# The attention's linear part as one matrix per batch, with a new order of the instructions

## The chip, the cores and the metric

The kernel runs on one core of a Trainium2 chip. Its engines are PE (TensorE, matrix products), DVE (VectorE), ACT (ScalarE), POOL (GpSimd) and SP (SyncE, which here only issues DMAs). Each engine works through its own instructions in order; semaphores make one wait for another. The metric is the device time of one execution in microseconds (us), the median of several runs.

## What is computed

Attention over pooled keys is followed by a feed-forward layer. Keys and values are the same 768 vectors of each batch; there are 4 batches of 12288 queries with 128 channels.

```python
kv_pool = kv.reshape(B, H // r, r, W // r, r, C).mean(axis=(2, 4))
k = v = kv_pool.reshape(B, -1, C) @ w_sr
s = (q @ k.transpose(0, 2, 1)) / sqrt(C)
a = exp(s - s.max(-1)); a /= a.sum(-1) + 1e-09
x = (a @ v).reshape(B * S, D)
h = x @ w_in
out = (h - tanh(h)) @ w_out
```

## The kernel before

The scores are small, so the kernel writes exp(s) as 1 + s + r2 and sums the three parts apart. The keys are centred first, so the 1 sums to nothing but the mean, which is taken into constants; the part in s is a linear map of q, the matrix M of a batch (values times keys, `Mn`); only r2 needs the 768 keys. The feed-forward layer is likewise expanded about the batch's mean: a slope matrix A (128x128), and a remainder that comes from products with `winr` and `Wr`.

The queries are cut into 96 tiles of 512, 24 for each batch. `attention(g)` and `feed_forward(g)` issue one tile's work:

- three products of scores into wide PSUM buffers (`big`, 128x1024, three buffers, which all wide products share), each followed by ACT's exp (`E`) and DVE's r2 = E - 1 - s;
- the sum of r2 over the keys: SP copies the first r2 to `rs` (line 794), POOL's DMA queue adds the other two to it (line 797, called an add below), and PE sums over partitions (line 802); from that ACT makes the scale `t` (line 822);
- `num`, in the narrow PSUM bank `x`: six half-precision products of the values with r2 (line 818) and three products for the linear part, M high with the rounded q, M low with it, and M high with q's rest `ql` (line 808);
- DVE multiplies `num` by `t` to `df` (line 829), POOL rounds it to `dr` (line 832) and takes the rest `dl` (line 858). A high and low times `dr`, and A high times `dl`, go to the bank `acc` (line 878);
- eight wide products `dr` by `winr` (line 889). Seven of them go to ACT (square, `u`) and DVE (`r`); the eighth goes to ACT (copy, `v`) and then POOL (`z`, `z`, `rp`, lines 903 and 907). Sixteen products with `Wr` go to `acc` (line 927), ACT adds the constant and writes the result `o` (line 938), and SP stores it.

A tile of a batch's last part also carries a share of the next batch's preparation (`keys`, `about_centre`): the keys are gathered by 15 DMAs on POOL's queue that add to `kvp` (line 366, called gathers below), centred, multiplied; M, A, `winr` and `Wr` are made anew.

The order is written out by numbers: each operation has a step (tile start `8 g` plus an offset from the table `AT`), and a planner sorts each engine's operations by step, within the dependencies. `BUFS` says how many buffers each name has.

Of the kernel before, what the change touches and what calls it, by code (L numbers as in the profile page):

```python
# [21 lines left out]
P = 128  # L22
# [134 lines left out]
def attention_then_ffn(ctx: ExitStack, tc: tile.TileContext, q, kv_by_key, kv_by_place, w_sr, w_in,  # L157
# [76 lines left out]
    def words_of(step, load_step, n, kind):  # L234
# [55 lines left out]
        Y, M, part = (ym, "y"), (ym, "m"), (key, n)  # L290
        plan.op(load_step, "SP", 0.5, load_words, () if kind == "i" else ("held",), (words,), late=2.0,
# [13 lines left out]
    def weights(step, load_step):  # L305
# [3 lines left out]
        for j in range(2):  # L309
            turned = f"turned.{j}"  # L310
            big(turned, step + NW + j)
            for k in range(2):
                def turn(j=j, k=k, turned=turned):
                    for f in range(8 * j + 4 * k, 8 * j + 4 * k + 4):
                        PE.matmul(out=plan[turned][:, (f % 8) * P : (f % 8 + 1) * P],
                                  lhsT=win32[:, f * P : (f + 1) * P], rhs=ident,
                                  start=True, stop=True)

                plan.op(step + NW + j, "PE", 1.0, turn, (("win32", 2 * j + k), "ident"),
                        ((turned, k),), late=0.2)  # L320
# [4 lines left out]
            plan.op(step + NW + j, "ACT", 1.03, copy, (turned,), (("winT", j),), late=0.1)  # L325
        s = 16.0
        bank("WW", "x", s)
        sb("WW32", "W2", [P, P])
        bank("W4", "x", s + 1)
# [11 lines left out]
        norm(s + 1, "WW32", "W4", B)  # L341
# [13 lines left out]
    def keys(b, s0):  # L355
# [6 lines left out]
        NK = K // KB  # L362
        for w in range(W if b else 0):
# [6 lines left out]
            at = (b * NG - GATHER[b - 1] + max(w - 1, 0)) * UN + AT["more"][0] - 2 * UN  # L370
            plan.op(at - (0.01 if w else 4), *(("POOL", 0.87) if w else ("SP", 0.5)), gather, (), (kvp,),
                    late=3.0, dma=1.0, lane=w > 0)
        for j in range(0 if b else NK):
# [3 lines left out]
            at = slice(j * KB, (j + 1) * KB)  # L377

            def load(at=at, key=key):
                SP.dma_start(out=plan[key], in_=kv_by_key[:, at, :])  # L380

            plan.op(s - 8, "SP", 0.5, load, (), (key,), late=2.0, dma=1.27)
            if j % 3 == 2:
                for k, w in enumerate((8, 4, 2, 1)):
                    def fold(key=key, w=w, at=at):
                        x = plan[key]
                        to = plan[kvp][:, at].unsqueeze(2) if w == 1 else x[:, :, 0:w]
# [4 lines left out]
            else:  # L392
                def pool(key=key, at=at):
                    V.tensor_reduce(out=plan[kvp][:, at], in_=plan[key], op=ALU.add, axis=AX.X)
# [8 lines left out]
        Mh = f"Mh.{b}"  # L403
        sb(Mh, "Mh", [P, 2, C], R32)
# [3 lines left out]
        for x, at in ((pc, s0), (pm, s3), (p4, s4)):  # L408
            bank(x, "x", at)
# [66 lines left out]
        def copy_moment():  # L476
            A.activation(out=plan[Mn], in_=plan[pm][:, 0:P], func=AF.Copy, scale=scale)
            A.copy(out=plan[Mh][:, 0], in_=plan[Mn])

        def moment_left():  # L480
            PL.tensor_tensor(out=plan[Mh][:, 1], in0=plan[Mn], in1=plan[Mh][:, 0].bitcast(F32),
                             op=ALU.subtract)

        for n in range(NK // 2):
            of = (kvp,) if b else ((kvp, 2 * n), (kvp, 2 * n + 1))
            plan.op(s0 - 0.5, "DVE", 0.3, partial(part, n), of, ((row, n),))
        plan.op(s0, "DVE", 0.35, mean, (row,), (row,))
        plan.op(s0, "ACT", 0.85, apart, (kvp, row), (kvp,), late=0.1)
        plan.op(s0, "PE", 0.2, centre, ("wsr", row), (pc,), late=0.2)
        plan.op(s0, "DVE", 0.12, copy_centre, (pc,), (cen,))  # L490
        for c in range(2):
            plan.op(s1 + c / 4, "PE", 0.65, partial(product, c), ("wsr", kvp), ((pk, c),), late=0.2)
        plan.op(s1, "ACT", 0.9, copy_keys, (pk,), (kTr,), late=0.1)
        for j in range(2):
            plan.op(s2 + j / 4, "PE", 0.7, partial(product_by_key, j), ("wsr", kvp), ((pv, j),),
                    late=0.2)
        plan.op(s2, "ACT", 0.85, copy_values, (pv,), (vv32,), late=0.1)
        plan.op(s2 + (0 if b else 2), "DVE" if b else "ACT", 0.9, small_values, (pv,), (vvr,))
        plan.op(s3, "PE", 1.8, moment, (vv32,), (pm,), late=0.2)
        plan.op(s3, "ACT", 0.65, copy_moment, (pm,), (Mn, Mh), late=0.1)  # L500
        plan.op(s3, "POOL", 0.35, moment_left, (Mn, Mh), (Mh,))
        norm(s4, Mn, p4, b)

    def about_centre(b, s0):
# [9 lines left out]
        sb(Am, "A", [P, C])  # L514
        Ah = f"Ah.{b}"
        sb(Ah, "Ah", [P, 2, C], R32)
        sb(Wr, "Wr", [P, FT, C], R32)
        FS, CS, AS, APART, SA, TA, WI, WS = EARLY if b < 2 else LATER
        first_at = [s0 + FS * n if b else s0 - 9.9 + n / 4 for n in range(4)]
        known = s0 + 3 * FS + 2 if b else s0 - 9  # L520
        winr_at = known + WI if b else s0
        slopes_at = [known + SA + AS * n if b else n / 2 - SL for n in range(4)]
        third_at = [known + TA + AS * (n + 0.5) if b else n / 2 - THIRD for n in range(4)]
        for n in range(4):
            if b or n == 0:
                bank(f"{ph}.{n}", "x" if b else "acc", first_at[n])
            if b:
                bank(f"{pa}.{n}", "x", slopes_at[n] + APART)
        if not b:
            bank(f"{pa}.0", "acc", slopes_at[0])  # L530
# [49 lines left out]
        def inverse_of():  # L580
            h, z, p, g0, g1, a3, slope, y, inv = (x(n) for n in range(9))
            V.reciprocal(out=inv, in_=slope)
            V.tensor_reduce(out=stat[:, b : b + 1], in_=z, op=ALU.add, axis=AX.X)
# [644 lines left out]
```

## Time and profile before

| | us |
|---|---|
| median of 3 runs (1326.55 to 1327.71) | 1327.05 |
| span of the profiled execution | 1326.8 |
| busy PE | 1271.4 |
| busy DVE | 1220.6 |
| busy ACT | 1197.4 |
| busy POOL | 1143.5 |

A busy share is no distance from a limit here: PE's matmuls overlap, so that its busy time holds waits too. The execution is best read in stages, with the start of the result copies `o` as a clock, one for each tile:

| stages | us | tiles |
|---|---|---|
| up to the second `o` | 100.7 | 1 |
| gather stages (one gather in nearly every tile) | 125.7, 125.5, 163.1 | 10, 10, 13 |
| change stages (the next batch is prepared) | 149.6, 152.3, 150.3 | 10, 11, 11 |
| plain stages (neither) | 146.7, 122.2 | 12, 10 |
| a check of the expansion's limits, between the plain stages | 42.4 | 3 |
| the end | 48.3 | 4 and the rest |

### The profile page before, as it was taken

To read this page: it belongs to the slowest core of one execution; us is meant where nothing else is said; L and a number is where in the kernel's file an instruction comes from. 1 tells how busy PE (TensorE), PEld (TensorE's weight loads), DVE (VectorE), ACT (ScalarE), POOL (GpSimd) and SP (SyncE) were. 2 spreads that over 40 slices of the span, in tenths; PEclk is the share of its full clock that TensorE was granted. 3 is DMA by queue.
4 is the path that set the end of the run, shared out by engine and by line. 5 is a ranking of instruction groups with operands and counts; after the bars stand their busy time and mean duration, and the time that the engine had idled before them with its cause. 6 is when DMAs were issued, how large, how long until landed. Compare 5 with 4: busy or idle time off the path is not lost.

```text
span 1326.8 us, 17379 instructions
## 1 busy us (share of the span) xinstructions
PE 1271.4 (96%) x5520; PEld 889.0 (67%) x5520; DVE 1220.6 (92%) x1201; ACT 1197.4 (90%) x1423; POOL 1143.5 (86%) x969
## 2 busy tenths in 40 slices
PE   4899999899899999999999999999999999999997
PEld 3666666676666667766666666776767667667665
DVE  6789999788899999999899999999999999899996
ACT  4689999788899999899899999899899999899996
POOL 3587999779999988799999998799998889798896
PEclk8899999999999999999999999999999999999999
DMA  9255666436566654445566664444444444434431
GB/s 350 52 112 128 139 134 141 94 106 129 125 136 140 134 128 97 114 112 132 115 142 133 136 137 110 104 104 112 104 108 107 104 119 96 103 97 108 115 82 40
DMA packets 82708, 158.47 MB, mean 119 GB/s; under 512 B 9936, under 2 KB 12112, under 8 KB 82608
## 3 DMA queue, kind: packets, MB, share of 16 engines
q0 software_dynamic: 33552, 66.99, 30.8%
q1 hardware_dynamic: 49056, 90.29, 19.4%
q8 instruction: 45, 0.74, 0.2%
q14 instruction: 55, 0.45, 0.1%
HBM read 57.93 MB, written 25.39 MB: 63 GB/s over the span
## 4 chain that ended last, share of the span: by engine, by line
POOL 44%; PE 38%; ACT 6%; issue 6%; DMA 2%; DVE 2%; SPq 0%; POOLq 0%; ACTq 0%; DVEq 0%
PE acc L927 11%; POOL rp L907 11%; PE big L889 10%; POOL z L907 10%; POOL rs L797 6%; PE big L774 5%; POOL z L903 4%; PE x L818 4%; POOL ql L812 3%; POOL dr L832 3%; ACT E L778 3%; PE x L808 2%; PE acc L878 2%; ACT v L900 2%; POOL kvp L366 1%
## 5 line engine op out<-in xcount | busy, mean ns | idle before, releaser
L896 DVE SCALAR_TENSOR_TENSOR r<-big,u 128x1024 fp32r<-128x1024 f32 x672 | 778.9, 1217 | 27.9 <-ACT u L893 27.5
L893 ACT ACTIVATE u<-big 128x1024 f32<-128x1024 f32 x672 | 662.4, 1034 | 34.3 <-PE big L889 23.4
L889 PE MATMUL big<-dr,winr 128*128 128x512 f32 x1536 | 510.4, 413 | 1.7 <-DVE r L781 0.9
L927 PE MATMUL acc<-r,Wr 128*128 128x512 f32 x1344 | 426.8, 409 | 0.6 <-DVE r L896 0.6
L781 DVE SCALAR_TENSOR_TENSOR r<-E,big 128x1024 f16<-128x1024 f32 x288 | 350.2, 1217 | 51.1 <-ACT E L778 48.0
L889 PEld LDWEIGHTS big<-dr,winr 128*128 128x128 f32 x1536 | 276.5, 188 | 97.0 <-DVE r L781 25.8
L778 ACT ACTIVATE E<-big 128x1024 f32<-128x1024 f32 x288 | 296.0, 1029 | 19.9 <-PE big L774 9.7
L927 PEld LDWEIGHTS acc<-r,Wr 128*128 128x128 f32 x1344 | 251.8, 188 | 65.1 <-DVE r L896 1.5
L907 POOL TENSOR_TENSOR rp<-z,v 128x1024 fp32r<-128x1024 f32 x96 | 273.5, 2849 | 0.2
L907 POOL TENSOR_TENSOR z<-z,v 128x1024 f32<-128x1024 f32 x96 | 248.7, 2590 | 4.3
L797 POOL DMA_DIRECT2D rs<-r x188 | 223.7, 1190 | 6.9 <-DVE r L896 4.7
L774 PE MATMUL big<-qr,kTr 128*128 128x512 f32 x576 | 198.2, 426 | 4.8 <-ACT qr L759 1.6
L832 POOL TENSOR_SCALAR dr<-df 128x512 fp32r<-128x512 f32 x96 | 69.8, 727 | 122.9 <-DVE df L829 115.4
L818 PE MATMUL x<-r,vvr 128*128 128x512 f16 x576 | 175.2, 387 | 0.0
L812 POOL TENSOR_TENSOR ql<-q,qr 128x512 fp32r<-128x512 f32 x96 | 164.5, 1714 | 6.0 <-ACT qr L759 6.0
L858 POOL TENSOR_TENSOR dl<-df,dr 128x512 fp32r<-128x512 f32 x96 | 164.8, 1716 | 0.0
L774 PEld LDWEIGHTS big<-qr,kTr 128*128 128x128 f32 x576 | 105.9, 191 | 44.7 <-DVE r L781 13.3
L903 POOL TENSOR_SCALAR z<-v 128x1024 f32<-128x1024 f32 x96 | 111.0, 1156 | 0.0
L900 ACT COPY v<-big 128x1024 f32<-128x1024 f32 x96 | 97.7, 1018 | 1.5 <-PE big L889 1.3
L938 ACT ACTIVATE o<-acc,At 128x512 f32<-128x512 f32 x96 | 65.7, 684 | 30.4 <-PE acc L927 29.7
L927 PE MATMUL acc<-rp,Wr 128*128 128x512 f32 x192 | 74.3, 469 | 17.8 <-POOL rp L907 14.6
L818 PEld LDWEIGHTS <-vvr 128*128 128x128 f16 x576 | 33.7, 99 | 79.8 <-issue 79.3
(184 smaller groups left out, 1008.5 us busy)
## 6 DMA issues: line engine op xcount, KB each, us to landing
rs<-r POOLq DMA_DIRECT2D x188, 256.0 KB, 3.9
q<-in_q_dram SPq DMA_DIRECT2D x96, 256.0 KB
out_dram<-o SPq DMA_DIRECT2D x96, 256.0 KB
rs<-r SPq DMA_DIRECT2D x94, 256.0 KB
kvp<-in_kv_by_place_dram POOLq DMA_DIRECT2D x45, 384.0 KB, 4.9
r<-in_kv_by_key_dram SPq DMA_DIRECT2D x6, 512.0 KB
kc<-inverse SPq DMA_DIRECT2D x12, 256.0 KB
u<-in_moe_w_in_dram SPq DMA_DIRECT2D x3, 512.0 KB
```

The lines of the kernel that those rows point to most:

```text
L774: PE.matmul(out=half(plan[s], h), lhsT=plan[kTr][:, n * P : (n + 1) * P], rhs=plan[qr], start=True, stop=True)
L778: A.activation(out=plan[e], in_=plan[s], func=AF.Exp)
L781: V.scalar_tensor_tensor(out=plan[r], in0=plan[e], scalar=-1.0, in1=plan[s], op0=ALU.add, op1=ALU.subtract)
L797: PL.dma_start(out=plan[rs], in_=plan[r2s[k]], accum_op=ALU.add)
L812: PL.tensor_tensor(out=plan[ql], in0=plan[qs], in1=plan[qr].bitcast(F32), op=ALU.subtract)
L818: PE.matmul(out=plan[num], lhsT=plan[vvr][:, n], rhs=half(plan[f"r2.{g}.{k}"], h), start=(start and h == 0), stop=(stop and h == 1))
L858: PL.tensor_tensor(out=plan[dl], in0=plan[df], in1=plan[dr].bitcast(F32), op=ALU.subtract)
L889: PE.matmul(out=half(plan[hp], h), lhsT=plan[winr][:, f * P : (f + 1) * P], rhs=plan[dr], start=True, stop=True)
L893: A.activation(out=plan[u], in_=plan[hp], func=AF.Square)
L896: V.scalar_tensor_tensor(out=plan[r], in0=plan[hp], scalar=1.0, in1=plan[u], op0=ALU.add, op1=ALU.mult)
L907: PL.tensor_tensor(out=plan[to], in0=plan[x], in1=plan[y], op=ALU.mult)
L927: PE.matmul(out=plan[acc], lhsT=plan[Wr][:, 2 * n + h], rhs=half(plan[r], h), start=(start and h == 0), stop=(stop and h == 1))
```

## The change

The slope matrix and the attention's matrix are joined: the kernel makes AM = M A / 768 once for each batch, and the linear part of attention and the linear part of the feed-forward layer become one map of q. In a tile:

- the three products of M with q before `df` become one, M rounded with the rounded q (`about`);
- before it ACT copies the values' sum out of the bank to `e` (`beside`), 128x512, rounded;
- the products into `acc` are AM high and low with the rounded q, AM high with `ql`, and A rounded with `e`: four in place of three;
- DVE's product with `t` is written rounded, straight to `dr`; `df`, POOL's `dr` and POOL's `dl` are gone;
- POOL makes y = q t (`shared_q`) and takes `ql` = y - rounded q, both after `t` is known; `t` is scaled by 768 in exchange for `winr` and A scaled down.

For each batch there is one more 128x128 product and two more small ACT copies (AM), and one small POOL operation less. The numbers of the order are all new; a table `MOVES` shifts single operations of the batches' preparation, and gathers and adds no longer keep a set order among themselves. `q` is held until `y` is made.

```diff
+    MOVES = {
+        "words.i.2": 48.8, "WW": 33.3, "W4": 70.9, "pool.0": 41.4, "pool.1": 78.7, "pool.2": 3.4,
...
+    def at(step, *name):
+        return step + MOVES.get(".".join(str(x) for x in name), 0.0)
...
-            plan.op(at - (0.01 if w else 4), *(("POOL", 0.87) if w else ("SP", 0.5)), gather, (), (kvp,),
-                    late=3.0, dma=1.0, lane=w > 0)
+            plan.op(put - (0.01 if w else 4), *(("POOL", 0.87) if w else ("SP", 0.5)), gather, (), (kvp,),
+                    late=3.0, dma=1.0)
...
+        def slopes_by_key():
+            A.activation(out=plan[Am], in_=plan[pt][:, 0:P], func=AF.Copy, scale=1.0 / K)
+            A.copy(out=plan[Au], in_=plan[Am])
+
+        def joined_slopes():
+            PE.matmul(out=plan[pt][:, P : 2 * P], lhsT=plan[Mn], rhs=plan[Am], start=True, stop=True)
+
+        def upper_joined():
+            A.copy(out=plan[Am], in_=plan[pt][:, P : 2 * P])
+            A.copy(out=plan[AM][:, 0], in_=plan[Am])
...
-        def straight(start, stop):
-            upper, lower = (plan[Mh][:, n] for n in range(2))
-            for n, (x, y) in enumerate(((upper, qr), (lower, qr), (upper, ql))):
-                PE.matmul(out=plan[num], lhsT=x, rhs=plan[y], start=(start and n == 0),
-                          stop=(stop and n == 2))
+        def shared_q():
+            PL.tensor_tensor(out=plan[y], in0=plan[qs], in1=plan[t], op=ALU.mult)
 
         def lower_q():
-            PL.tensor_tensor(out=plan[ql], in0=plan[qs], in1=plan[qr].bitcast(F32),
+            PL.tensor_tensor(out=plan[ql], in0=plan[y], in1=plan[qr].bitcast(F32),
                              op=ALU.subtract)
...
+        def beside():
+            A.copy(out=plan[e1], in_=plan[num])
+
+        def about():
+            PE.matmul(out=plan[num], lhsT=plan[Mu], rhs=plan[qr], start=False, stop=True,
+                      skip_group_check=True)
...
-            A.activation(out=plan[t], in_=plan[den], func=AF.Copy, scale=-1.0 / K**2,
-                         bias=1.0 / K)
+            A.activation(out=plan[t], in_=plan[den], func=AF.Copy, scale=-1.0 / K,
+                         bias=1.0)
...
-            V.tensor_tensor(out=plan[df], in0=plan[num], in1=plan[t], op=ALU.mult)
-
-        def rounded():
-            PL.tensor_scalar(out=plan[dr], in0=plan[df], scalar1=1.0, scalar2=1.0, op0=ALU.mult,
-                             op1=ALU.mult)
+            V.tensor_tensor(out=plan[dr], in0=plan[num], in1=plan[t], op=ALU.mult)
...
-        def lower_left():
-            PL.tensor_tensor(out=plan[dl], in0=plan[df], in1=plan[dr].bitcast(F32), op=ALU.subtract)
...
-            upper, lower = (plan[Ah][:, n] for n in range(2))
-            for n, (x, y) in enumerate(((upper, dr), (lower, dr), (upper, dl))):
+            upper, lower = (plan[AM][:, n] for n in range(2))
+            for n, (x, y) in enumerate(((upper, qr), (lower, qr), (upper, ql), (plan[Au], e1))):
                 PE.matmul(out=plan[acc], lhsT=x, rhs=plan[y], start=(start and n == 0),
-                          stop=(stop and n == 2))
+                          stop=(stop and n == 3))
```

Where the order moves, three places. First POOL in a gather stage, one tile before (`rs` is an add, `kvp` a gather):

```order
L832 TENSOR_SCALAR dr<-df 128x512
L903 TENSOR_SCALAR z<-v 128x1024
L366 DMA kvp<-in_kv_by_place_dram 128x768
L907 TENSOR_TENSOR z<-z,v 128x1024
L797 DMA rs<-r_870 128x1024
L907 TENSOR_TENSOR rp<-z,v 128x1024
L858 TENSOR_TENSOR dl<-df,dr 128x512
L812 TENSOR_TENSOR ql<-q,qr 128x512
L797 DMA rs<-r_904 128x1024
```

And POOL in the same batch after the change, a tile with one gather inside and the next one's gather:

```order
L833 DMA rs<-r_864 128x1024
L842 TENSOR_TENSOR y<-q,t 128x512
L845 TENSOR_TENSOR ql<-y,qr 128x512
L391 DMA kvp<-in_kv_by_place_dram 128x768
L833 DMA rs<-r_854 128x1024
L936 TENSOR_SCALAR z<-v 128x1024
L940 TENSOR_TENSOR z<-z,v 128x1024
L940 TENSOR_TENSOR rp<-z,v 128x1024
L391 DMA kvp<-in_kv_by_place_dram 128x768
L833 DMA rs<-r_1000 128x1024
```

An add stood between `z` and `rp` and two operations on `dr` on the way; now `z`, `z`, `rp` stand together, both adds stand ahead of them with `y` and `ql` between, and a gather can stand directly ahead of an add.

Second ACT in a plain stage, one tile before (`x` in `t<-x` is the bank of sums):

```order
L893 ACTIVATE u<-big 128x1024 x3
L759 CAST qr<-q 128x512
L893 ACTIVATE u<-big 128x1024 x2
L822 ACTIVATE t<-x 128x512
L893 ACTIVATE u<-big 128x1024 x2
L778 ACTIVATE E<-big 128x1024
L938 ACTIVATE o<-acc,At 128x512
L778 ACTIVATE E<-big 128x1024
L900 COPY v<-big 128x1024
L778 ACTIVATE E<-big 128x1024
```

And ACT in a plain stage after:

```order
L926 ACTIVATE u<-big 128x1024 x2
L862 ACTIVATE t<-x 128x512
L926 ACTIVATE u<-big 128x1024 x3
L971 ACTIVATE o<-acc,At 128x512
L814 ACTIVATE E<-big 128x1024 x2
L855 CAST e<-x 128x512
L933 COPY v<-big 128x1024
L926 ACTIVATE u<-big 128x1024
L814 ACTIVATE E<-big 128x1024
L926 ACTIVATE u<-big 128x1024
L795 CAST qr<-q 128x512
```

The copy `e` is new, between two exps and `v`; the rest is the same eleven wide operations and three narrow ones, in another sequence.

Third PE where the second batch's mean is used (`row` and `col`), before:

```order
L927 MATMUL acc<-r,Wr 128x512 x2
L889 MATMUL big<-dr,winr 128x512 x2
L440 MATMUL x<-row,wsr 128x1
L808 MATMUL x<-qr,Mh 128x512 x2
L808 MATMUL x<-ql,Mh 128x512
L774 MATMUL big<-qr,kTr 128x512 x2
```

And after:

```order
L810 MATMUL big<-qr,kTr 128x512 x2
L922 MATMUL big<-dr,winr 128x512 x2
L468 MATMUL x<-row,wsr 128x1
L911 MATMUL acc<-qr,AM 128x512 x2
L911 MATMUL acc<-ql,AM 128x512
L911 MATMUL acc<-e,Au 128x512
L564 MATMUL x<-col,win_67 128x1 x4
L922 MATMUL big<-dr,winr 128x512 x2
```

The product with the mean was followed by M's products into the same bank; now the four products into `acc` follow it. It also comes some six tiles earlier in the batch.

## Rows read from the trace of the kernel before

**Rows 1.** Stretches, cut just before a start of the result copy of line 938, with that line's instructions alone: length, busy ACT (and the count, which is that of the tiles), granted clock of TensorE, DMA share, GB/s. In order: a gather and a change stage three times, then the two plain stages.

```profile
100.70:226.40 125.70, 6.87 (x10) 1.00 0.62 135
226.40:376.00 149.60, 6.84 (x10) 0.99 0.52 117
376.00:501.50 125.50, 6.88 (x10) 1.00 0.62 134
501.50:653.80 152.30, 7.51 (x11) 1.00 0.47 113
653.80:816.90 163.10, 8.94 (x13) 1.00 0.62 134
816.90:967.20 150.30, 7.51 (x11) 1.00 0.43 104
967.20:1113.90 146.70, 8.14 (x12) 1.00 0.44 108
...
1156.30:1278.50 122.20, 6.80 (x10) 1.00 0.42 104
```

**Rows 2.** The last plain stage with all instructions: length, busy PE, PEld, DVE, ACT and POOL, each with its count, then clock and DMA.

```profile
1156.30:1278.50 122.20, 122.20 (x521) 85.14 (x521) 121.55 (x111) 119.99 (x141) 105.76 (x81) 1.00 0.42 104
```

**Rows 3.** The chain of work that ended last, in order of time (start, us, what), over one tile of a gather stage, without its pieces of issue below 0.2 us.

```profile
704.09 0.69 ACT o L938
704.78 0.72 ACT E L778
...
705.58 1.02 ACT v L900
706.60 0.93 ACT E L778
...
707.65 0.62 POOL dr L832
708.26 1.01 POOL z L903
709.28 0.42 POOL kvp L366
...
709.85 2.70 POOL z L907
712.55 0.84 POOL rs L797
713.39 2.45 POOL rp L907
...
715.88 0.74 PE acc L927 x2
```

**Rows 4.** The timeline of ACT in a plain stage: start, us (first start to last end), operation, count.

```profile
1217.44 0.68 ACT L938 ACTIVATE o<-acc,At 128x512 f32<-128x512 f32 x1
1218.01 1.02 ACT L778 ACTIVATE E<-big 128x1024 f32<-128x1024 f32 x1
...
1223.90 0.60 ACT L759 CAST qr<-q 128x512 fp32r<-128x512 f32 x1
1224.40 1.94 ACT L893 ACTIVATE u<-big 128x1024 f32<-128x1024 f32 x2
1226.22 0.61 ACT L822 ACTIVATE t<-x 128x512 f32<-128x512 f32 x1
1226.70 1.05 ACT L893 ACTIVATE u<-big 128x1024 f32<-128x1024 f32 x1
```

**Rows 5.** The timeline of PE in the same tile.

```profile
1227.38 0.63 PE L808 MATMUL x<-qr,Mh 128*128 128x512 f32 x2
1227.85 0.40 PE L808 MATMUL x<-ql,Mh 128*128 128x512 f32 x1
1228.08 0.39 PE L774 MATMUL big<-qr,kTr 128*128 128x512 f32 x1
```

**Rows 6.** The timeline of DVE in the same tile.

```profile
1220.20 0.68 DVE L829 TENSOR_TENSOR df<-x,t 128x512 f32<-128x512 f32 x1
1220.93 1.22 DVE L781 SCALAR_TENSOR_TENSOR r<-E,big 128x1024 f16<-128x1024 f32 x1
1222.09 8.05 DVE L896 SCALAR_TENSOR_TENSOR r<-big,u 128x1024 fp32r<-128x1024 f32 x7
```

**Rows 7.** Groups of PE's instructions by line in the second change stage (busy us, mean ns, idle before): the four largest that belong to the preparation of a batch (four smaller ones follow).

```profile
L685 PE MATMUL x<-Wg,wout 128*128 128x129 f32 x32 | 4.3, 275 | 0.0
L536 PE MATMUL x<-col,win 128*128 128x1 f32 x32 | 3.8, 239 | 0.0
L456 PE MATMUL big<-wsr,kvp 128*128 128x128 f32 x12 | 1.6, 284 | 0.0
L447 PE MATMUL big<-kvp,wsr 128*128 128x384 f32 x4 | 1.6, 512 | 0.0
```

**Rows 8.** In the first change stage, the timeline of PE where the batch's mean is used (in brackets the idle time before and what ended it), and the stretch behind it (length, busy PE, granted clock, DMA).

```profile
239.50 0.35 PE L440 MATMUL x<-row,wsr 128*128 128x1 f32 x2 [2.97 <-DVE row L433]
240.50:244.30 3.80, 3.70 (x10) 0.57 0.40 69
```

**Rows 9.** DMAs issued by POOL, from the page: count, KB, median us from issue to landing.

```profile
rs<-r POOLq DMA_DIRECT2D x188, 256.0 KB, 3.9
kvp<-in_kv_by_place_dram POOLq DMA_DIRECT2D x45, 384.0 KB, 4.9
```

More of the change, by code (lines that the diff above doesn't have):

```diff
@@ L407, in keys @@
         s4 = s4 if b else 24.0
-        for x, at in ((pc, s0), (pm, s3), (p4, s4)):
-            bank(x, "x", at)
+        sc, s1, s2, s3, s4 = (at(x, "keys", n, c) for n, x in enumerate((s0, s1, s2, s3, s4)))
+        sv = [at(x, "keys", n, c) for n, x in (("1b", s1 + 0.25), ("2b", s2 + 0.25))]
+        for x, put in ((pc, sc), (pm, s3), (p4, s4)):
+            bank(x, "x", put)
         if b == 0:
@@ L477, in copy_moment @@
             A.activation(out=plan[Mn], in_=plan[pm][:, 0:P], func=AF.Copy, scale=scale)
[L478 to L482, printed above, removed]
+            A.copy(out=plan[Mu], in_=plan[Mn])
         for n in range(NK // 2):
             of = (kvp,) if b else ((kvp, 2 * n), (kvp, 2 * n + 1))
-            plan.op(s0 - 0.5, "DVE", 0.3, partial(part, n), of, ((row, n),))
@@ L487, in keys @@
[L487 to L490, printed above, removed]
+            plan.op(sc - 0.5, "DVE", 0.3, partial(part, n), of, ((row, n),))
+        plan.op(sc, "DVE", 0.35, mean, (row,), (row,))
+        plan.op(sc, "ACT", 0.85, apart, (kvp, row), (kvp,), late=0.1)
+        plan.op(sc, "PE", 0.2, centre, ("wsr", row), (pc,), late=0.2)
@@ L496, in keys @@
                     late=0.2)
-        plan.op(s2, "ACT", 0.85, copy_values, (pv,), (vv32,), late=0.1)
-        plan.op(s2 + (0 if b else 2), "DVE" if b else "ACT", 0.9, small_values, (pv,), (vvr,))
+        plan.op(sv[1], "ACT", 0.85, copy_values, (pv,), (vv32,), late=0.1)
+        plan.op(at(s2 + (0 if b else 2), "small", c), "DVE" if b else "ACT", 0.9, small_values, (pv,), (vvr,))
         plan.op(s3, "PE", 1.8, moment, (vv32,), (pm,), late=0.2)
-        plan.op(s3, "ACT", 0.65, copy_moment, (pm,), (Mn, Mh), late=0.1)
@@ L501, in keys @@
-        plan.op(s3, "POOL", 0.35, moment_left, (Mn, Mh), (Mh,))
+        plan.op(s3, "ACT", 0.65, copy_moment, (pm,), (Mn, Mu), late=0.1)
         norm(s4, Mn, p4, b)
@@ L728, in attention_then_ffn @@
+        plan.op(joined, "POOL", 0.35, lower_joined, (Am, AM), (AM,))
     AT = dict(
[L729 to L735 removed]
@@ L736, in attention_then_ffn @@
-        copied=-18.59, added=[-15.50, -11.66],
-        shares=-7.54, left=-6.81, straight=-6.02, apart=-2.72, rounded=-2.20, rounded_q=-24.34,
-        slope=4.93, result=11.47, lower_q=-12.50, lower_left=2.65)
+        forth=[3.6, 1.8, 8.5, 1.26, 5.1, 1.18, 0.8, 5.9],
+        first=[7.0, 3.66, 9.3, 2.7, 7.07, 2.66, 1.8, 8.2],
+        then=[12.1, 2.8, 8.3, 2.6, 5.8, 1.8, 0.6, 7.9],
+        back=[10.1, 8.81, 9.4, 5.39, 8.7, 3.9, 3.1, 9.2], scores=[-18.6, -21.3, -21.74],
+        exps=[-16.9, -18.5, -19.8], beyond=[-18.0, -20.3, -20.7], values=[-5.5, -6.1, -5.0],
@@ L740, in attention @@
+        more=[12.4, 14.8], num=-6.5, copied=66.9, added=[-7.6, -4.6], shares=-7.0, left=-5.7,
+        beside=-1.7, about=-2.8, apart=-2.3, rounded_q=-23.4, slope=7.9, result=11.7, shared_q=9.2,
+        lower_q=10.5)
     def attention(g, s0):
         b, i = divmod(g, NG)
-        kTr, vvr, Mh = (f"{x}.{b}" for x in ("kTr", "vvr", "Mh"))
-        qs, qr, dl, dr, den, num, t = (f"{x}.{g}" for x in ("q", "qr", "dl", "dr", "den", "num", "t"))
+        kTr, vvr, Mu = (f"{x}.{b}" for x in ("kTr", "vvr", "Mu"))
@@ L790, in attention @@
         bank(den, "x", s0 + AT["shares"])
-        bank(num, "x", s0 + min(AT["straight"], *AT["values"]))
+        bank(num, "x", s0 + AT["num"])
         def copied():
```

140 lines of the change are left out of this document (73 added, 67 removed), and 15 rows, old and new, of the table MOVES.

## The prediction

> **What bounds the kernel now.** I read the stretches between result copies first, then the engines' sums in the stretch that is nothing but tiles, then the chain of waits where a tile takes longer than that.
>
> The stretches [rows 1] show three paces. The two plain stages make 22 tiles in 268.9 us, 12.22 each; the three gather stages 33 tiles in 414.3, 12.55 each; the three change stages 32 tiles in 452.2, 14.13 each. The chip does the same tile each time, so the second and third pace are what something else costs: 33 x 0.33 = 10.9 us and 32 x 1.91 = 61 us.
>
> In a plain stage nearly everything is full. DVE is busy 121.55 of 122.20 us, 12.16 for each of 10 tiles [rows 2]. Three of PE's matmuls take 1228.08 - 1227.38 = 0.70 us from start to start [rows 5], 0.233 each, so that its 52 of 512 columns are 12.1 us. ACT is busy 12.00, but some of that is waiting inside instructions: start to start, two squares take 1.82 us [rows 4], so 11 wide operations are 10.0; with o 0.57, qr 0.50 and t 0.48 that makes 11.56. POOL is busy 10.58 [rows 2]. DVE and PE set this pace together, and POOL has room.
>
> In a gather stage the chain goes round once in a tile [rows 3]: o, E, v, E on ACT, then dr, z, the gather, z, the add and rp on POOL, then PE's last product into acc, which the next o waits for. These pieces sum to 12.14 us, and small issue gaps bring it to 12.55. No engine is full in it; it is a loop of waits that is longer than DVE's work.
>
> In the change stages POOL has this loop and the next batch's preparation. One place is different: PE stood 2.97 us for DVE's mean, and behind that its granted clock was 0.57 over 3.80 us [rows 8], between the levels of 1.2 and 2.4 GHz.
>
> **The change part by part, for one tile.** PE loses one matmul net (three of M become one, three of the slopes four): 51 x 0.233 = 11.9 us. A shorter PE alone gives nothing, since DVE is next at 12.16.
>
> DVE keeps its eleven instructions; the product with t only writes a rounded result, of the same size as the 0.73 us that df takes from start to start [rows 6]. Nothing there.
>
> ACT gains e, a 512-column copy out of PSUM. The trace has no such copy; its nearest rows are t with 0.48 and o with 0.57 [rows 4]. A price below zero is excluded, since nothing leaves ACT. I take 0.48, because e has fixed factors as t has, where o adds a column. ACT's floor becomes 12.04 to 12.13. The Trainium skill (ScalarE: Activation LUTs, section What ACT_TABLE_LOAD costs) states 186 ns and 0.833 ns for each column for an ACTIVATE with immediate factors, and about 93 ns of overlap with the next one; as an estimate from that page e is 0.52 us and the floor 12.08. The row of t is below that page's figure, and the floor stays under DVE's 12.16 by either.
>
> POOL loses dr (0.62 us [rows 3]) and dl, and gains y, a product of the same size as dl: 10.58 - 0.62 = 9.96 us.
>
> The loop of the gather stage is cut in two. dr does not pass POOL any more, and no add stands between the z's and rp. What is left: o 0.69, E 0.72, a second E 0.91, e 0.48, v 1.02, z 1.01, z 2.70, rp 2.45, acc 0.74, and the 0.4 us of issue: 11.1 us, or 11.5 with a gather inside [rows 3, 4]. Both are shorter than DVE's 12.16, so DVE is late next.
>
> With DVE full, the three wide buffers come next. From DVE's start on a buffer to its earliest start on that buffer's next content pass: its own 1.22, PE's two matmuls 0.74, ACT's 1.05 [rows 3, 4, 6], and three hand-offs of some 0.03: 3.1 us. Three squares' turns on DVE are 3 x 1.14 = 3.42 (6.83 us for the six steps of x7 [rows 6]) and hide it. Two turns and the product with t are 1.16 + 1.14 + 0.73 = 3.03 and leave 0.07 open. I take 12.16 + 0.07 + 0.02 = 12.25 us a tile, in plain and gather stages alike.
>
> The new waits: e must follow the last product of the values, and `about` must follow e, in the same bank. Four pairs of matmuls stand between (4 x 0.47 = 1.9 us) and cover e's 0.6; if ACT is late by more than a microsecond, PE stands, and all wide products behind it. y needs t and therefore ql comes late, but ql is used only in the fourth product into acc; q is held longer, while SP's load of it has most of a tile. I cost these at nothing.
>
> The adds: the second now waits for the first to land, with y and ql (2.5 us, two products of dl's kind) between. An add lands after 3.9 us [rows 9], so POOL stands about a microsecond, of the 2.2 it has to spare. Where a gather stands directly ahead of the first add, which the order has in some 15 tiles, landing takes between 3.9 and 4.9 + 3.9 - 0.8 = 8.0 us; add, z, z, rp and gather are 0.84 + 1.01 + 2.70 + 2.45 + 0.42 = 7.4. The sum is 11.3 to 15.4, against 12.25. I take 6 us, as the gather has a part of its 4.9 behind it: 13.4, and since rp may come over 1 us late before PE waits, 4 us in all for these tiles.
>
> The change stages: PE's preparation is 4.3 + 3.8 + 1.6 + 1.6 = 11.3 us for a batch [rows 7], and four smaller groups, which I put at 2 together. PE has 12.25 - 11.9 = 0.35 us to spare in each of about 11 tiles, 3.9 us. So 7.4 to 9.4 us are left for each change of batch; I take 9. Now they cost 452.2 - 32 x 12.22 = 61, or 20 each, because POOL's loop was already longer than the tile. POOL's part hides in its 2.3 us of room. The bounds for one change are 4 (most of PE's part hides too) and 20 (nothing is won). The new order puts four products into acc where PE stood for the mean.
>
> Head, check stage and end I leave as they are, with 3 us either way: the first keys' loads and the last tiles have no new bound.
>
> **Sum.** Gather stages 33 x 12.25 = 404.3 for 414.3: -10.0. Plain 22 x 12.25 = 269.5 for 268.9: +0.6. Change stages 32 x 12.25 + 27 = 419.0 for 452.2: -33.2. Gathers ahead of adds +4. Together -38.6 on a span of 1326.8, so 1288.2; the median of the runs is 0.25 above the span, so 1288.
>
> **The rivals.** 1. *ACT becomes the bound.* In a plain tile ACT now takes 12.22 for 11.56 of work, 0.66 of waits for PE and hand-offs. If it keeps these, a tile takes 12.04 + 0.66 = 12.70, with o's price for e 12.79. Over the 87 tiles of the three kinds that is 39 to 47 us above my 12.25: 1327 to 1335, slower. It decides from 12.69 us a tile on (38.6 / 87 = 0.44). For it speaks that the whole chain of ACT has no gap in [rows 4]; against it that most of these waits are ACT waiting for PE, which becomes shorter.
>
> 2. *The adds behind gathers hold POOL.* The loop just worked out with 6 us and no cover costs 15 x 1.15 = 17 us, 13 more than I counted: 1301; at 8 us it is 15 x 3.15 = 47, and the gather loop is merely replaced: 1331. The Trainium skill (DMA: Bandwidth & Descriptors, section Two DMAs through the same engine are not ordered) states that descriptors of one queue start in order, which puts the add's data behind the gather's. By that rule the time is nearer to 1301 than to 1288; no row here has a gather directly ahead of an add.
>
> 3. *The change stages win little*, because PE's preparation comes in pieces of 2 us that the three buffers can't bank, and DVE's in pieces of 1 us: 15 us each for my 9 gives 1306; 20 gives 1321.
>
> 4. *DVE alone is the bound* (12.17) and a change costs 5: 87 x 0.08 + 12 + 4 = 23 us less, 1265.
>
> **How the numbers follow.** Forecast, 1275 to 1298: 0.60. Rivals 2 and 3, 1298 to 1320: 0.22. Rival 1 with a tile of 12.6 and more: 0.13, of which 0.04 lies within 0.2% (2.7 us, about what a measurement can tell from no change) and 0.09 is slower. Rival 4: 0.05. Faster 0.60 + 0.22 + 0.05 = 0.87. The range leaves out the slow half of rival 1 and most of rival 4: 1266 to 1318.
>
> **What would show it.** Plain and gather stages at the same 12.2 to 12.3 us a tile; no chain through dr or through rp, but one that passes through DVE and PE; ACT busy above 12.0 a tile with under 0.3 us of idle; POOL under 10.1 in a plain tile, and waiting for adds to land; change stages with 8 to 10 us above their tiles, and no half clock at the mean. Wrong would be: a plain tile above 12.5 with ACT never idle (rival 1), POOL's adds landing after 6 us with PE waiting for rp (rival 2), or change stages still above 13.5 us a tile (rival 3).

## The result, and the profile after

| | before | after | forecast |
|---|---|---|---|
| median, us | 1326.80 | 1334.77 (1333.17 to 1336.98, 4 runs) | 1288 |
| ratio to before | 1 | 1.0063 [1.0049, 1.0077] | 0.971 |
| span of the profiled execution | 1326.8 | 1331.5 | 1288.2 |
| busy PE, DVE, ACT, POOL | 1271.4, 1220.6, 1197.4, 1143.5 | 1264.0, 1224.9, 1231.7, 1100.6 | |

The kernel became 0.6% slower, outside the range of 1266 to 1318. One execution, of the kernel with the new arithmetic in the old order below, took 3124.2 us with all its matmuls slower; it is left out, and with it that kernel's only profile.

First the stretches of the kernel after, cut at the starts of its result copies (line 971 now), over the same tiles as [rows 1]: length, busy ACT of that line (count, that of the tiles), granted clock, DMA share, GB/s. In order: three times a gather and a change stage, then the two plain stages.

```profile
95.05:235.85 140.80, 6.84 (x10) 0.99 0.52 117
235.85:375.05 139.20, 6.87 (x10) 0.98 0.63 139
375.05:507.85 132.80, 6.84 (x10) 0.99 0.46 109
507.85:656.95 149.10, 7.53 (x11) 0.99 0.60 136
656.95:825.85 168.90, 8.87 (x13) 1.00 0.47 111
825.85:966.55 140.70, 7.51 (x11) 1.00 0.45 112
966.55:1116.05 149.50, 8.17 (x12) 1.00 0.43 106
1156.15:1279.85 123.70, 6.80 (x10) 1.00 0.43 107
```

The change stages gained 10, 3 and 10 us on [rows 1]. The gather stages, which were to gain 10 together, lost 15, 7 and 6, and the plain tile went from 12.22 to 12.36 (by the starts themselves; the stretch shown is cut to 0.05 us). The new order has put a part of the preparation into the gather stages, so a gather and a change stage are best read together: 280.0, 281.9 and 309.6 us now for 275.3, 277.8 and 313.4.

What a long tile holds is seen in one of 18.1 us. Its stretch with all instructions (length; busy PE, PEld, DVE, ACT, POOL with counts; granted clock; DMA), then PE's timeline inside it (in brackets the idle time before and what ended it), then POOL's, then the start of the chain that ended last in it (start, us, what):

```profile
250.40:268.50 18.10, 15.04 (x52) 10.02 (x51) 13.16 (x13) 12.77 (x16) 16.30 (x13) 0.81 0.77 159
```

```profile
261.90 1.01 PE L838 MATMUL x<-rs,share 128*128 128x512 f16 x2 [3.06 <-DMA rs<-r]
...
263.57 1.05 PE L960 MATMUL acc<-r,Wr 128*128 128x512 f32 x2
264.42 1.05 PE L922 MATMUL big<-dr,winr 128*128 128x512 f32 x2
```

```profile
250.75 0.88 POOL L833 DMA_DIRECT2D rs<-r  x1 [0.63 <-DMA rs<-r]
...
254.28 0.89 POOL L391 DMA_DIRECT2D kvp<-in_kv_by_place_dram  x1
256.23 0.86 POOL L833 DMA_DIRECT2D rs<-r  x1 [1.06 <-DMA rs<-r]
```

```profile
250.75 5.18 DMA rs<-r
...
256.23 5.64 DMA rs<-r
```

The first add is issued at 250.75, and POOL stands 1.06 us until it has landed, after 5.18 us, and the second one may go, at 256.23, directly behind a gather. PE stands 3.06 us at the product with `rs`, which starts when the second add has landed, after 5.64 us. Behind the stand two matmuls take 264.42 - 263.57 = 0.85 us, 0.43 each for the 0.233 of [rows 5]: the granted clock is at its lower level of 1.2 GHz, and over the tile it is 0.81. Over the first two gather and change stages (95 to 657 us) the view of waits has of this pair (total, times, longest, us):

```profile
POOL rs L833 <- DMA rs<-r: 30.0, 19, 2.6
...
PE x L838 <- DMA rs<-r: 13.7, 11, 3.1
```

A second kind of stand is in the chain of work that ended last, in order of time (start, us, what), in the first batch: DVE's part of the mean (`row`) waits for the last gather, issued at 147.75, and DVE's whole row waits behind it. The second fence is this wait in the view of waits over the whole execution.

```profile
147.75 4.76 DMA kvp<-in_kv_by_place_dram
...
152.53 0.04 DVE row L456
```

```profile
DVE row L456 <- DMA kvp<-in_kv_by_place_dram: 4.5, 1, 4.5
```

### The profile page after: what moved, and what is told of

It reads as the page before. It is cut to its first block, busy times and chain, and to the rows that moved or that the text cites. A ratio compares the mean times of both kernels' runs of the same rounds, so it can differ in the third digit from the quotient of the medians.

```text
span 1331.5 us, 17137 instructions
## 1 busy us (share of the span) xinstructions
PE 1264.0 (95%) x5432; PEld 863.2 (65%) x5432; DVE 1224.9 (92%) x1205; ACT 1231.7 (93%) x1527; POOL 1100.6 (83%) x869
## 4 chain that ended last, share of the span: by engine, by line
PE 67%; POOL 9%; DMA 9%; DVE 6%; issue 4%; ACT 4%; SPq 0%; POOLq 0%; ACTq 0%; DVEq 0%
PE big L922 22%; PE acc L960 19%; DMA rs<-r 7%; PE big L810 7%; PE x L851 7%; PE acc L911 5%; DVE r L929 4%; POOL z L940 3%; PE x L838 3%; POOL rp L940 2%; ACT u L926 2%; DVE r L817 1%; POOL z L936 1%; PE x L858 1%; POOL rs L833 1%
## 5 line engine op out<-in xcount | busy, mean ns | idle before, releaser
L922 PE MATMUL big<-dr,winr 128*128 128x512 f32 x1536 | 523.0, 422 | 7.2 <-DVE r L929 5.0
L960 PE MATMUL acc<-r,Wr 128*128 128x512 f32 x1344 | 442.7, 411 | 1.7 <-ACT o L971 1.2
L922 PEld LDWEIGHTS big<-dr,winr 128*128 128x128 f32 x1536 | 265.8, 190 | 141.1 <-DVE r L929 32.5
L940 POOL TENSOR_TENSOR rp<-z,v 128x1024 fp32r<-128x1024 f32 x96 | 231.5, 2411 | 7.2
L940 POOL TENSOR_TENSOR z<-z,v 128x1024 f32<-128x1024 f32 x96 | 230.4, 2400 | 8.0
L833 POOL DMA_DIRECT2D rs<-r x188 | 174.0, 925 | 60.9 <-DMA rs<-r 39.1
L842 POOL TENSOR_TENSOR y<-q,t 128x512 f32<-128x512 f32 x96 | 159.1, 1657 | 0.0
L845 POOL TENSOR_TENSOR ql<-y,qr 128x512 fp32r<-128x512 f32 x96 | 124.2, 1294 | 7.4
L851 PEld LDWEIGHTS <-vvr 128*128 128x128 f16 x576 | 33.7, 98 | 78.3 <-issue 77.8
L862 ACT ACTIVATE t<-x 128x512 f32<-128x512 f32 x96 | 58.4, 608 | 22.8 <-issue 19.0
L838 PE MATMUL x<-rs,share 128*128 128x512 f16 x188 | 57.2, 386 | 22.6 <-DMA rs<-r 19.3
```

The costliest lines, as they stand in the source:

```text
L833: PL.dma_start(out=plan[rs], in_=plan[r2s[k]], accum_op=ALU.add)
L842: PL.tensor_tensor(out=plan[y], in0=plan[qs], in1=plan[t], op=ALU.mult)
L851: PE.matmul(out=plan[num], lhsT=plan[vvr][:, n], rhs=half(plan[f"r2.{g}.{k}"], h), start=(start and h == 0), stop=(stop and h == 1))
L922: PE.matmul(out=half(plan[hp], h), lhsT=plan[winr][:, f * P : (f + 1) * P], rhs=plan[dr], start=True, stop=True)
L940: PL.tensor_tensor(out=plan[to], in0=plan[x], in1=plan[y], op=ALU.mult)
L960: PE.matmul(out=plan[acc], lhsT=plan[Wr][:, 2 * n + h], rhs=half(plan[r], h), start=(start and h == 0), stop=(stop and h == 1))
```

## The experiments

Twelve kernels ran. Those without gathers, with small gathers, with gathers aside, without `e` and with a square ahead of `v` have one execution each; the four of the kernel after lie within 3.8 us. The stages of some of the profiled executions, from the starts of its result copies (us; "prep" is what the 65 tiles of the three batches take above the plain tile of the same kernel; it holds the preparation, and with gathers also their cost):

| kernel | plain tile | first two batches' gather stages | prep | time |
|---|---|---|---|---|
| before | 12.22 | 125.6, 125.5 | 72 | 1326.8 |
| after | 12.36 | 140.8, 132.8 | 68 | 1334.8 |
| after without gathers | 12.36 | 134.3, 129.0 | 34.5 | 1295.5 |
| after, gathers even, preparation as before | 12.36 | 127.0, 123.6 | 57 | 1318.4 |
| the same, gathers ahead of adds | 12.36 | 138.6, 136.9 | 104 | 1368.0 |
| before, DVE writes dr | 12.23 | 122.5, 122.4 | 48 | 1302.3 |
| the same, a product less | 12.23 | 122.5, 122.5 | 44 | 1298.3 |

**What the gathers cost.** Theory A: an add directly behind a gather lands late, and PE and POOL stand for it (the prediction's rival 2). Rival B: the pieces of the preparation make the long tiles.

```diff
-                if w:
-                    PL.dma_start(out=plan[kvp], in_=kv_by_place[b - 1, w], accum_op=ALU.add)
-                else:
+                if not w:
                     SP.dma_start(out=plan[kvp], in_=kv_by_place[b - 1, w])
```

> The changed kernel in its own order, without the 45 gathers that add to the pooled keys: the keys of batches 2 to 4 are those of one place only. Theory A (an add that stands directly behind a gather in POOL's queue lands some 2 us late, PE stands for it at the product with rs, and its clock halves behind that): the long tiles of 14 to 18 us in the first three batches go down to 12.4 to 13.6, and the time to 1285 to 1300. Rival B (the long tiles come from the pieces of the next batch's preparation and the three wide buffers): long tiles stay, 1320 or more. Either way the plain tiles stay at 12.36.

Measured: 1295.49, span 1293.8, so the gathers cost 37.7 us of 1331.5. The stretches (as above) of the three batches, 20, 21 and 24 tiles:

```profile
90.95:352.75 261.80, 13.70 (x20) 1.00 0.43 107
352.75:622.35 269.60, 14.27 (x21) 1.00 0.44 108
622.35:928.85 306.50, 16.33 (x24) 1.00 0.44 107
```

Against 65 x 12.36 = 803.4 that leaves 34.5 us of preparation. Two long tiles of 15.8 and 16.4 us stay in the first batch; in the second PE stands at the same product for a copy of the preparation, not for an add. B holds for these two, and for four of 13.8 to 14.5 us that stay as well. That bytes matter, not only issues, was tried with the gathers cut to an eighth:

```diff
-                    PL.dma_start(out=plan[kvp], in_=kv_by_place[b - 1, w], accum_op=ALU.add)
+                    PL.dma_start(out=plan[kvp][:, 0:96], in_=kv_by_place[b - 1, w][:, 0:96],
+                                 accum_op=ALU.add)
```

> The changed kernel in its own order, each of the 45 gathers adding 96 of the 768 columns (so that the keys are wrong): as many issues on POOL, an eighth of the bytes. If the gathers' bytes ahead of the adds in the queue make the stands: near the run without gathers, 1294 to 1300. If their issue time on POOL (0.4 to 0.9 us each) or the order of landings does: 1315 or more.

Measured: 1304.33, span 1302.6. Of the 37.7 us 28.9 go with the bytes and 8.8 stay, so the number lies between the two expectations, nearer to the first.

**Where a gather may stand.** The first attempt moved the gathers in POOL's row of the kernel after, and nothing else:

```diff
         order.sort()
...
+        order = self.behind_adds(order)
```

> The changed kernel with 24 or so gathers moved in POOL's row alone: one that stood directly ahead of an add now stands behind the tile's second add, and a second one of that tile behind the first z. Theory A: adds land after 3.3 to 4 us again, PE's stands of 1 to 3.5 us at the product with rs go, 1295 to 1308. Rival C (the gathers' bytes slow the adds wherever they stand, or POOL's whole row is too long there): 1320 to 1335.

Measured: 1350.38, ratio 1.0177 [1.0153, 1.0202]: worse, so as an argument for A this failed. DVE's timeline of that kernel in the first batch shows why:

```profile
163.61 0.86 DVE L483 TENSOR_REDUCE row<-kvp 128x4 f32<-128x128 f32 x4 [10.19 <-DMA kvp<-in_kv_by_place_dram]
```

A gather that is issued later lands later, and the mean, which the new order puts early, now stops DVE for 10.19 us; that tile takes 22.5. Over the whole execution DVE's waits for the last gathers rose from 4.5 us to 14.6, while POOL's waits for a transfer into `rs` fell from 39.1 us to 25.8 and PE's from 19.3 to 11.6: the adds held the engines less, as A has it, and the mean cost more. So both had to be changed at once: one gather a tile, and the later batches' preparation back at its old steps.

```diff
-        "turn.0": 42.8, "gather.1.1": -24.4, "gather.1.2": 18.0, "gather.1.6": -6.4,
...
-            put = at((b * NG - GATHER[b - 1] + max(w - 1, 0)) * UN - 17.0, "gather", c, w)
+            put = at((b * NG - GATHER[b - 1] + max(w - 1, 0)) * UN - 12.5, "gather", c, w)
...
-                    late=3.0, dma=1.0)
+                    late=3.0, dma=1.0, lane=w > 0)
```

> The changed kernel with its own tile steps, but one gather a tile in POOL's row behind the tile's second add, and the preparation of batches 2 to 4 at the steps of the kernel before (all its shifts taken out). If the gathers cost 38 us because the early preparation crowds them: gather tiles 12.4 to 12.6, no stands at rs, 1295 to 1315. If POOL's row of the new tile (two adds with 2.9 us between them) can't bear a gather anywhere: gather tiles above 13, 1320 or more.

Measured: 1318.36, ratio 0.9925 [0.9901, 0.9949]. The gather tiles are what was expected (12.36, but for one of 15.8 that holds a piece of preparation and is as long without gathers); the total is 3 us above, with 57 us for the preparation at its old steps. Then the same kernel with the gathers directly ahead of the first add; PE's row is the same, and four small operations of the preparation moved in DVE's and ACT's.

```diff
-            put = at((b * NG - GATHER[b - 1] + max(w - 1, 0)) * UN - 12.5, "gather", c, w)
+            put = at((b * NG - GATHER[b - 1] + max(w - 1, 0)) * UN - 15.6, "gather", c, w)
```

> As the run with one gather a tile behind the second add, each gather now directly ahead of the tile's first add; only POOL's row differs. That run had gather tiles of 12.36 and 1318. If an add directly behind a gather is enough to hold PE (the prediction's rival 2): first adds land after 5.5 to 6 us, gather tiles 13 to 15, 1335 to 1390. If the place alone costs little and it is the early preparation that crowds the gathers: gather tiles up to 12.5, 1317 to 1322.

Measured: 1367.97, ratio 1.0291 [1.0261, 1.0321], 50 us above the even gathers by the place alone. One fence for each of the two: a stretch of gather tiles with all instructions (columns as above), 9 tiles of the even kernel and 6 of this one; then the chain that ended last in one such tile of this one (start, us, what).

```profile
377.00:488.15 111.15, 110.90 (x460) 73.24 (x459) 109.31 (x102) 110.99 (x136) 98.97 (x71) 1.00 0.61 133
```

```profile
395.65:477.85 82.20, 74.99 (x307) 49.78 (x306) 73.27 (x67) 74.62 (x90) 66.56 (x50) 1.00 0.56 125
```

```profile
408.42 6.04 DMA rs<-r
414.47 0.29 issue
414.75 0.88 POOL rs L817
415.64 1.09 POOL z L920
...
416.81 2.37 POOL z L924
...
419.25 0.25 POOL rp L924
...
421.59 0.59 POOL kvp L375
422.18 6.14 DMA rs<-r
```

A tile takes 111.15 / 9 = 12.35 there and 82.20 / 6 = 13.70 here. The chain goes round on POOL without PE: the add lands after 6.04 us, the second add may go, then z, z, rp, the next gather, the next add, 422.18 - 408.42 = 13.76 us. A holds.

How much of the gathers' cost is the mean's wait was asked of a kernel without `e` (below, 1339.25), since only it has room for a tile beside `kvp`:

```diff
-                    PL.dma_start(out=plan[kvp], in_=kv_by_place[b - 1, w], accum_op=ALU.add)
+                    PL.dma_start(out=aside, in_=kv_by_place[b - 1, w], accum_op=ALU.add)
```

> As the run without e (1337), but the 45 gathers add to a tile that nothing reads, so that the next batch's mean waits for none of them (its keys are those of one place); bytes and places in POOL's row are the same. If most of the gathers' 38 us is the mean's wait for the last one: 1300 to 1312. If it is the adds behind gathers: 1325 to 1337.

Measured: 1329.25, span 1327.4 for 1337.4. Of these 10.0 us 1.6 lie in the check stage, where there is no gather, and the view of waits has DVE wait for a gather once without `e`, 4.9 us in the first batch. So the mean's wait is some 5 to 8 us there, from one execution of each, and the adds behind gathers are the larger part.

**Was the loop through dr real?** The kernel before, with that part of the change alone:

```diff
-            V.tensor_tensor(out=plan[df], in0=plan[num], in1=plan[t], op=ALU.mult)
+            V.tensor_tensor(out=plan[dr], in0=plan[num], in1=plan[t], op=ALU.mult)
...
-            PL.tensor_scalar(out=plan[dr], in0=plan[df], scalar1=1.0, scalar2=1.0, op0=ALU.mult,
-                             op1=ALU.mult)
...
-            PL.tensor_tensor(out=plan[dl], in0=plan[df], in1=plan[dr].bitcast(F32), op=ALU.subtract)
+            PL.tensor_tensor(out=plan[dl], in0=plan[dr].bitcast(F32), in1=plan[dr].bitcast(F32), op=ALU.subtract)
```

> The kernel before, in its own order, with one part of the change alone: DVE writes its product with t rounded, straight to dr, and POOL's rounding is gone; dl becomes dr minus dr, zeros, so A's product with the rest counts nothing. If the loop through dr on POOL was what the gather and change stages waited for, as the prediction had it: gather tiles go from 12.56 to 12.2 to 12.3, change tiles from 14.1 to 13.0 to 13.6, 1285 to 1305. If the loop closes elsewhere (the add between the z's and rp): gather tiles 12.5, 1320 or more.

Measured: 1302.28, ratio 0.9815 [0.9798, 0.9831]. Its stretches (as above), the first gather and change stage, the second gather stage and the last plain stage:

```profile
98.05:220.45 122.40, 6.79 (x10) 1.00 0.63 138
220.45:364.25 143.80, 6.82 (x10) 0.99 0.53 121
364.25:486.65 122.40, 6.80 (x10) 1.00 0.62 137
1129.35:1251.65 122.30, 6.80 (x10) 1.00 0.42 104
```

A gather tile costs what a plain tile costs, 12.24 and 12.23. In this order a gather stands between the two z's, and the next add 3.3 us behind it [rows 3]. Then one product of PE's 52 and POOL's dl less:

```diff
-            PL.tensor_tensor(out=plan[dl], in0=plan[dr].bitcast(F32), in1=plan[dr].bitcast(F32), op=ALU.subtract)
+            pass
...
-            for n, (x, y) in enumerate(((upper, dr), (lower, dr), (upper, dl))):
+            for n, (x, y) in enumerate(((upper, dr), (lower, dr))):
...
```

> The kernel before with DVE writing dr (as in the run before in which dl was zeros), and the product with dl and POOL's dl left out: the same result as that run's, PE with 51 products a tile for 52, every other instruction at its place. If PE's room beside DVE hides the preparation of a batch, as the prediction's sum had it: plain and gather tiles stay at 12.22, each change stage gains 2 to 4 us, 1290 to 1297. If the preparation is paid in full wherever it comes in pieces of 1 us and more: 1300 to 1303, as with the product.

Measured: 1298.29, ratio 0.9783 [0.9766, 0.9799], the fastest kernel here with all of the gathers, and 2.7% below the kernel after. The change stages are 142.4, 146.4 and 146.3 for 143.7, 147.8 and 147.2, a gain of 1.2 on average, for the 2 to 4 expected: room on PE hides less of the preparation than the prediction's sum had it.

**What makes the plain tile 12.36?**

```diff
-            A.copy(out=plan[e1], in_=plan[num])
+            pass
...
-            for n, (x, y) in enumerate(((upper, qr), (lower, qr), (upper, ql), (plan[Au], e1))):
+            for n, (x, y) in enumerate(((upper, qr), (lower, qr), (upper, ql), (plan[Au], qr))):
```

> The changed kernel in its own order without ACT's copy e: the fourth product into acc takes the rounded q instead, so that PE does as much. If e's time on ACT makes the plain tile's 12.36 (the forecast was 12.25): plain tiles at 12.15 to 12.25, 1318 to 1324. If PE, DVE and the wide buffers make it: plain tiles stay within 0.04 of 12.36, 1328 to 1332.

Measured: 1339.25. The last plain stage of 10 tiles of the kernel after, then of this one (columns as above):

```profile
1156.15:1279.85 123.70, 123.38 (x512) 81.32 (x511) 121.22 (x111) 123.50 (x151) 102.57 (x71) 1.00 0.43 107
1161.95:1285.55 123.60, 123.60 (x512) 81.09 (x511) 122.25 (x111) 119.78 (x141) 102.55 (x70) 1.00 0.43 107
```

12.36 again, with ACT 3.7 us less busy than in the kernel after: e is not it. The span became 5.9 us longer in other places (up to the second `o` 2.8, in the three batches 1.5, in the check 1.4); the cause is open, and 3.8 us is what executions of the kernel after differ by. Next the square that DVE waits for behind dr, moved ahead of v:

```diff
-        forth=[3.6, 1.8, 8.5, 1.26, 5.1, 1.18, 0.8, 5.9],
-        first=[7.0, 3.66, 9.3, 2.7, 7.07, 2.66, 1.8, 8.2],
+        forth=[5.1, 1.8, 8.5, 1.26, 3.6, 1.18, 0.8, 5.9],
+        first=[7.07, 3.66, 9.3, 2.7, 7.0, 2.66, 1.8, 8.2],
```

> The changed kernel with two wide products changed about in its table of steps: the square whose r DVE takes behind dr is made ahead of v on ACT (and its product ahead of v's on PE). In a plain tile DVE stands 0.25 us behind dr for that square, which ACT makes after two exps, e and v. If this place in ACT's row sets the plain pace: 12.15 to 12.25 a plain tile and no idle time of DVE there. If the loop of the three wide buffers sets it wherever the square stands: 12.33 to 12.40. The rest of the order is planned anew by it, so only plain tiles are compared.

Measured: 1379.09, with tiles up to 36 us in the batches, whose order came out otherwise. Its plain tile is 123.7 / 10 = 12.37, so this place does not set it either.

**The new arithmetic in the old order.**

```diff
-        forth=[3.6, 1.8, 8.5, 1.26, 5.1, 1.18, 0.8, 5.9],
+        forth=[3.94, 1.06, 1.67, 5.41, 0.16, 6.02, 6.63, -0.46],
...
-        beside=-1.7, about=-2.8, apart=-2.3, rounded_q=-23.4, slope=7.9, result=11.7, shared_q=9.2,
-        lower_q=10.5)
+        shares=-7.54, left=-6.81, beside=-3.4, about=-3.0, num=-5.3, apart=-2.72,
+        rounded_q=-24.34, slope=5.5, result=11.47, shared_q=2.65, lower_q=3.5)
```

> The changed kernel's arithmetic in the order of the kernel before: its table of tile steps (y and ql where dl and ql stood, about and e around the values' end), no shifts of the later batches' preparation, and one gather a tile between the z's, in POOL's row. If the new order is what lost the time (adds close together with gathers ahead of them, preparation early): gather and plain tiles 12.2 to 12.3, change stages 13 to 16 above their tiles, 1285 to 1305. If the new arithmetic itself costs it (e on ACT, y behind t): tiles of 12.4 and more, 1315 to 1340.

Measured: 1399.09 to 1403.59 in four executions, ratio 1.0555 [1.0533, 1.0578]. It ran again, with the values' products earlier:

```diff
-        beyond=[-19.46, -20.25, -18.25], values=[-3.75, -5.26, -4.35],
+        beyond=[-19.46, -20.25, -18.25], values=[-4.60, -6.05, -5.25],
...
-        shares=-7.54, left=-6.81, beside=-3.4, about=-3.0, num=-5.3, apart=-2.72,
+        shares=-7.54, left=-6.81, beside=-3.6, about=-3.0, num=-6.1, apart=-2.72,
```

> As the run with the new arithmetic in the old order, with the products of the values 0.85 of a step earlier, so that four products stand between the last of them and the product that waits for e. If PE's wait for e right behind the values made that run's 1400: 1290 to 1320. If the old order does not bear e at all (e and v ahead of the exps on ACT): 1380 or more.

Measured: 1381.21, ratio 1.0405 [1.0385, 1.0426]. The chain of one of its plain tiles:

```profile
1277.10 0.68 ACT o L957
1277.78 0.92 ACT E L800
1278.70 0.15 ACT e L841
1278.85 0.20 issue
1279.04 1.06 ACT v L919
...
1280.14 0.73 PE big L908 x2
...
1289.74 0.48 PE acc L946 x2
...
1290.26 0.68 ACT o L957
```

A loop of 1290.26 - 1277.10 = 13.16 us: o, E, e and v on ACT, then PE's row from the product that v makes room for to the last one into acc, which the next o waits for. In the old row `e` stands in a loop that goes round once in a tile. It has 0.35 us of it (0.15 and the 0.20 behind it), so it does not make the whole 0.94 us above the old plain tile of 12.22; what makes the rest was not tried. So the old order doesn't bear the new arithmetic as it stands; the gain of writing dr on DVE (1302.3) needs none of it.

## Why the prediction was wrong, point by point

**The failed step** is "Where a gather stands directly ahead of the first add": its loop was worked out as 13.4 us with the add landing after 6, and then written down to "4 us in all for these tiles", "since rp may come over 1 us late before PE waits". The loop itself was right: 13.70 a tile and 6.04 us to land in the kernel with the gathers ahead of the first adds. The write-down was wrong in three ways. The loop closes on POOL (add, add, z, z, rp, gather, add), so lateness adds up from tile to tile and a slack is used up once, not in each tile. PE waits more for `rs`, where nothing was allowed (19.3 us in the kernel after), than for `rp` (7.2 us). And 28 of the adds have a gather directly ahead, 17 of them first adds and 11 second ones, where I counted some 15 first ones alone. The gathers cost 37.7 us for my 4. At the price of the place alone (49.6 us for 42 adds, 1.18 each) 28 adds come to 33 us, by estimate, and the mean's wait is of the size of the rest.

This was rival 2, which the prediction priced at 1301 (landing after 6 us) to 1331 (after 8 us) and gave 0.22 together with rival 3. The Trainium skill (DMA: Bandwidth & Descriptors, section Two DMAs through the same engine are not ordered) states that descriptors of one queue start in order, from which the prediction put the add's data behind the gather's. The runs agree: 6.04 us behind 384 KB, and 28.9 of the 37.7 us gone with an eighth of the bytes. That the result lies in rival 1's 1327 to 1335 is chance, as the plain tile shows below.

**The mean's wait for the last gather** had no term. The new order has the mean "some six tiles earlier in the batch", and the prediction asked what PE does there, not when the gathers, which the mean needs, could have landed. It is one wait of 4.5 us of DVE in the kernel after, and some 5 to 8 us in the kernel without `e`.

The ledger, from the forecast's span of 1288.2:

| term | forecast | measured | difference |
|---|---|---|---|
| tile of three batches and plain stages | 12.25 | 12.36 | 87 x 0.11 = +9.6 |
| gathers | 4 | 1331.5 - 1293.8 = 37.7 | +33.7 |
| preparation of three batches | 27 | 34.5 (without gathers) | +7.5 |
| head, check, a piece in the first plain stage, end | 0 | -9.7, -2.2, +1.2, +3.3 (without gathers) | -7.4 |
| sum | | | +43.4, 1331.6 for 1331.5 |

**The pace of a plain tile**, forecast 12.25 with DVE full, is 12.36. ACT, PE and DVE in the kernel after's plain tile, one fence each (columns as in [rows 4 to 6]):

```profile
1218.60 1.93 ACT L814 ACTIVATE E<-big 128x1024 f32<-128x1024 f32 x2
1220.41 0.60 ACT L855 CAST e<-x 128x512 fp32r<-128x512 f32 x1
1220.88 1.05 ACT L933 COPY v<-big 128x1024 f32<-128x1024 f32 x1
1221.78 1.08 ACT L926 ACTIVATE u<-big 128x1024 f32<-128x1024 f32 x1
```

```profile
1223.84 0.40 PE L911 MATMUL acc<-e,Au 128*128 128x512 f32 x1
1224.26 0.70 PE L922 MATMUL big<-dr,winr 128*128 128x512 f32 x2
```

```profile
1221.96 0.69 DVE L869 TENSOR_TENSOR dr<-x,t 128x512 fp32r<-128x512 f32 x1
1222.89 1.23 DVE L929 SCALAR_TENSOR_TENSOR r<-big,u 128x1024 fp32r<-128x1024 f32 x1 [0.24 <-ACT u L926]
```

The prices were right: e takes 1220.88 - 1220.41 = 0.47 for the 0.48 taken, and a rounded dr costs DVE no more (0.69 for 0.68). The stand is where the prediction put it, at the turns beside the product with t: DVE waits 0.24 there, and PE 0.42 from start to start for 0.233. The "0.07 open" was mis-sized: it measured 0.24, and with DVE's 12.12 of busy time in a tile that is the 12.36. Rival 1 looks confirmed by ACT, which is never idle, but falls: without e the tile is the same. With the square moved ahead of `v` the tile is 12.37 still, so which turn of the three wide buffers sets it is open; the kernel after and these two, with three different rows of ACT, agree to 0.01.

**Right:** the loop through dr. With DVE writing `dr` (and POOL's row shorter by it), the three gather stages of the kernel before lost 10.3 us (125.6, 125.5, 163.2 to 122.5, 122.4, 159.1) for the 10.0 of the forecast, and a gather tile came to the plain tile's pace, 12.24.

**The change stages** were to cost 9 each; without gathers they cost 11.5 (34.5 / 3), so most of the gain is there. In the old order they cost 16 with `dr` on DVE (48 / 3), near rival 3's 15, and 19 in the new tile with the old preparation (57 / 3, with even gathers). The early preparation thus earns some 22 us (57 to 34.5); with it, and with the gathers where the new order has them, the gathers cost 38.

**The change taken apart:** writing `dr` on DVE is worth 25 us alone. By the ledger the new kernel has a gain of that size too, and gives it back to adds behind gathers, the mean's wait and a plain tile that is 0.14 us longer.

## What to carry to other kernels

A loop that is longer than the tile costs its whole excess in each tile: slack hides it once, so it belongs in the sum in full, with the row on which it closes named. Transfers that wait for each other on one queue want distance in the row of the engine that issues them: in the old kernel with `dr` on DVE 38 adds issued 2.5 to 4 us behind a gather landed after a median of 3.65 us. One large transfer put directly ahead of a small one that the matrix engine waits for cost 1.3 us a tile, and nothing behind it. Before work is moved earlier, ask when its last input lands, and try the parts of a large change alone: one part of this one, put into the old kernel, gained 25 us where the whole lost 8.

## What the runs showed of the hardware

An add of 256 KB landed 6.04 us after its issue directly behind a gather of 384 KB (the median of 42 such adds, and 5.8 of the 28 in the kernel after), for a median of 3.4 over all adds of the kernel after; with gathers of 48 KB the 28 adds directly behind one had a median of 3.6. With the gather behind the add it is the gather that lands later, after a median of 5.9 us for 4.8 ahead of it, and no engine waited more than 0.5 us for it there. A stand of PE of 3.06 us cost more than itself: its matmuls took 0.43 us for 0.233 from 262.4 to about 268 us, and the tile was 5.7 us longer than the same tile without gathers (12.40).
